# Softmax head steps: reciprocal of the row sums posted five half-steps later, the second projection copy recorded behind the exponentials, projection stores posted three half-steps sooner in the lead-in

## The chip, the cores and the metric

The kernel runs on one core of one Trainium2 chip. The metric is the device time of one execution in microseconds (us), the median of three runs. A profiled execution of the same program gives the span, the engines' busy times and every instruction's place; it is a fourth execution, with a time of its own. Engines are called as in the profile: PE (matmuls), PEld (its weight loads), DVE, ACT, POOL, and SP, which issues all the DMAs here.

## The reference

Four layers on x of 2048 x 640 in fp32, each added to its input: attention, Fourier mixing, attention, Fourier mixing.

```
def _A_ref(x, wqkv, wo):
    H = 32; Dh = D // H; W = 256
    qkv = (x @ wqkv).reshape(B, S, 3, H, Dh).transpose(2, 0, 3, 1, 4)
    ...
    scores = jnp.where(mask[None, None], scores, -1e9)   # 0 <= i - j < W
    p = _softmax(scores, axis=-1)
    o = jnp.einsum("bhqk,bhkd->bhqd", p, v)
    return o.transpose(0, 2, 1, 3).reshape(B, S, D) @ wo
def _B_ref(x, ...):   # Real(DFT_seq(DFT_hidden(x))) by four real matrices
    ...
x = x + _A_ref(_layernorm(x), A_wqkv, A_wo)
x = x + _B_ref(_layernorm(x), ...)
```

and the last two lines once more. The head width is 20, and a query sees the 256 keys up to its own.

## The kernel before

Every fp32 product is split into a high and a low part and made of three matmuls. The program is written out by hand: each engine executes its instructions in the order in which the Python code records them, and waits only where data or a buffer is not ready. All that the change touches lies in the attention layers, so it happens twice (about 126 to 620 us and 1240 to 1735 us of the profile).

**Head steps.** `heads` walks over 8 quads (four heads each) of 16 query blocks of 128 rows: 128 steps, with 10 steps of lead-in, numbered -10 to 128. A step has two half-steps, z = 0 and z = 1 (two heads each). Step t makes, for query block t + 10, the scores whose row maxima DVE takes (`s_head`, L548, and L553); for key block t, the transposed scores with the maximum folded in (`t_head`, L573), their exponentials on ACT (L582) and the window masks on POOL (L588, L592); and for block t - 1 the product with v (`pv`, L603). After every fourth block `finish` has the row sums of the exponentials gathered by a small DMA into `sm` (L623), DVE takes their reciprocal (L626), and a DMA stores it in `r_d` (L629), from where it is later read, broadcast, to scale the heads' outputs.

**Fill.** Between the heads' matmuls of z = 0 and z = 1 `fill` gives PE other work, taken in one sequence: first the q and k projections of the coming quads (`pieces`, L188 with 128x512 results), then 16 tiles of the output projection's first part (`partials`, L188 with 128x320 results, added up at L847), then 16 tiles of its second part (`late`, L170, added at L934 and L940). What the head steps have not done of it `after_heads` does afterwards, mixed with the first matmuls of the Fourier layer (`unit`, L1220). The second sequence can't begin before its first inputs are loaded and scaled: `prepare` asks at each step whether the reciprocals of quad 5, block 0 are stored (`others`, `self.stored`, set in `store`), and then loads, multiplies (L769) and splits (L163) them over the next 10 half-steps; until that is done (`made`, `early_o` in `more`), and once the projections are used up, a step has no fill at all.

**Copies.** A finished pair of projection results stands in PSUM banks 6 and 7 (`heavy`); `relieve` has ACT copy one to SBUF (L472, 128x512). One half-step later POOL makes the high part (L473), two half-steps later the low part (L474), and six half-steps later SP stores both in `qk_d` (L453). The destination `c` has three buffers, so a fourth cast waits until the first store has landed.

**Posting.** `post(d, fn)` puts an instruction off by d half-steps; `tick`, at the end of a half-step, records what has come due. So a delay is a place in the order, not a time.

Of the kernel before, what the change touches and what calls it, by code (L numbers as in the profile page):

```python
# [23 lines left out]
NQ = H // 4  # L24
# [37 lines left out]
class Net:  # L62
# [393 lines left out]
    def pieces(self, c, sbs, role):  # L456

        w = self.turn["w", c]
        sets, of = [], {}
        for sb in sbs:  # L460
            xt = self.xnt(sb)
            if sb % 2 == 0:
                sets.append(([], []))
            p = self.bank(role)
            of[id(p)] = p, sb, self.last_bank
            sets[-1][0].append(p)
            sets[-1][1].append([((w[:, 0, k, :], w[:, 1, k, :]), (xt[:, 0, k, :], xt[:, 1, k, :])) for k in range(KC)])

        def copied(p, sb):
            st = self.work.tile([P, 2, 512], F32R, name="c", tag="c", bufs=3)  # L470
            r = self.raw()[:, :512]
            self.nc.scalar.activation(r, p, AF.Copy)  # L472
            self.post(1, lambda: self.nc.gpsimd.tensor_copy(st[:, 0, :], r))  # L473
            self.post(2, lambda: self.nc.gpsimd.tensor_tensor(  # L474
                out=st[:, 1, :], in0=r, in1=st[:, 0, :].bitcast(F32), op=OP.subtract))
            self.post(6, lambda: self.store_qk(c, sb, st))
        for r in self.lockstep(sets):
            if isinstance(r, tuple):
                for p in r[1]:
                    p, sb, k = of[id(p)]  # L480
                    self.heavy.append((k, lambda p=p, sb=sb: copied(p, sb)))
                r = 0
            yield r
# [33 lines left out]
    def heads(self, xsrc, xdst, hook):  # L517
# [7 lines left out]
        def defer(d, fn):  # L525
            later.setdefault(now[0] + d, []).append(fn)
# [3 lines left out]
        def load_v(n):  # L530
            if n < 4 * NQ:
                nc.sync.dma_start(self.vq[n % 3][:, :384].rearrange("p (t c) -> p t c", c=96),
                                  self.vd[n // 4][:, n % 4 * 4:n % 4 * 4 + 4, :])
# [84 lines left out]
        def finish(quad, bk, ou):  # L618
            sm = pool.tile([P, 16], F32, name="sm", tag="sm")
            rc = pool.tile([P, 16], F32, name="rc", tag="rc")  # L620
            cols = slice(bk * 512, (bk + 1) * 512)
            at = (2, 7, 9) if quad < NQ - 1 else (1, 5, 6)
            self.post(at[0], lambda: nc.sync.dma_start(sm, ou[0:P:32, :]))  # L623
            self.post(at[0], lambda: nc.sync.dma_start(
                self.od[4 * quad:4 * quad + 4, :, cols].rearrange("h r s -> (h r) s"), ou))
            self.post(at[1], lambda: nc.vector.reciprocal(out=rc, in_=sm))  # L626

            def store():
                nc.sync.dma_start(  # L629
                    self.rd[bk, 4 * quad:4 * quad + 4, :].rearrange("h (a b) -> (h a) b", b=16), rc)  # L630
                self.stored.add((quad, bk))
            self.post(at[2], store)
# [15 lines left out]
        def relieve():  # L648
            while self.heavy:
                self.relieve()  # L650

        def more():

            r = next(self.proj, None)
            if r is not None:
                done[0] += r
                return r
            if not made[0] and self.early_o[0]["left"]:
                return None
            r = next(self.out, None)  # L660
            if r is not None:
                made[0] += r
                return r
            return next(self.rest, None) if self.left or self.ready_late() else None

        def fill(n):

            k, size = 0, 1
            while k < size:
                r = more()  # L670
                if r == 0 and k == 0:
                    continue
                if r != 1:
                    return
                k += 1
                if k == 1:
                    left = self.left + 1
                    size = -(-left // max(1, round(left / n)))
            if self.left == 0:
                more()  # L680
                relieve()

        load_v(0)
        load_v(1)
# [1 line left out]
        for step in range(-LEAD, steps + 1):  # L686
            now[0] = step
            self.wide, self.lead, self.tiled = step + LEAD > steps, step < -2, step < steps - 1
            for f in later.pop(step, []):
                f()  # L690
            s, t, v = step + LEAD, step, step - 1
            if due and s >= due[0][0]:
                while done[0] < due[0][1]:
                    fill(15)
                due.pop(0)
                q, j = (s + AHEAD) // 16, (s + AHEAD) % 16 // 4
                for i, f in enumerate(self.pack(q, j)):
                    defer(i // 3, f)
                for f in later.pop(step, []):
                    f()  # L700
            if v >= 0 and v % 4 == 3:
                load_v(v // 4 + 2)
            if done[0] < total:
                nf = max([FIRST if t < 0 else RATE]
                         + [(d - done[0]) / max(1, at - s) for at, d in due])
            elif made[0] < early:
                nf = LATE
            else:
                nf = LATE
            rows = ((s - 1) // 16, ((s - 1) % 16) // 4) if 4 <= s < steps + 4 and s % 4 == 0 else None  # L710
            for z in range(2):
                for e in range(2):
                    heads = [(t_head, t, e), (s_head, s, 1 - e)]
                    for head, n, i in heads[::-1] if e else heads:
                        if 0 <= n < steps:
                            head(n // 16, n % 16, z, i)
                if 0 <= t < steps:
                    for e in range(2):
                        t_exp(t // 16, t % 16, z, e, e + 1)
                    t_mask(t // 16, t % 16, z)  # L720
                if z:
                    if 0 <= v < steps:
                        pv(v // 16, v % 16)
                    if rows:
                        m_rows(*rows)
                if z == 0 and t >= 0 or t < -1 or t >= steps:
                    fill(nf)
                self.tick()
            if step >= steps:
                self.load_to(step - steps + 2)  # L730
            if step > 16 * (NQ - 1):
                self.poll_late(step - 16 * (NQ - 1))
# [794 lines left out]
```

## Time and profile before

| | us |
|---|---|
| median of 3 runs (lowest, highest) | 2259.83 (2257.31, 2260.46) |
| the profiled execution's own time | 2260.54 |
| its span, first to last instruction | 2258.8 |
| PE, DVE, ACT, POOL busy in the span | 2169.5, 1489.8, 1114.2, 1014.9 |
| mean granted TensorE clock | 0.987 |

The span is 1.7 us short of that execution's time. A row of the windows view is a stretch in us, its length, then for each engine its busy time with the count of instructions, then the granted TensorE clock as a part of full speed (PEclk), the DMA engines' busy share, and GB/s. A row of the timeline is start, length, engine, line, operation, names and count, and in brackets how long the engine was idle before it and what ended that. The ends of matmuls are modelled, so a busy PE need not be at its peak.

### The profile page before, as it was taken

The page shows a single profiled execution, that of the slowest core. Times are in us where ns is not written, and L with a number is a line of the kernel's source. Part 1 is how long each engine was busy: PE and PEld are TensorE (multiplying, and loading weights), DVE is VectorE, ACT ScalarE, POOL GpSimd, SP SyncE. Part 2 cuts the span into 40 slices and gives each one's busy share as a digit, 9 for nine tenths or more (in the row PEclk, how much of TensorE's full clock was granted, in tenths as well). Part 3 has the DMA queues.
Part 4 walks back from the last instruction along what each step waited for, and adds up shares of the span by engine and source line. Part 5 has one row for each costly group of instructions (what it writes and reads, how often), then busy time and mean ns, then how long its engine had stood idle before and what let it go on. Part 6 is the DMA issues. An engine that isn't in the chain of part 4 may idle for free. (4 is left out here: it accounts for less than half of the span.)

```text
span 2258.8 us, 49233 instructions
## 1 busy us (share of the span) xinstructions
PE 2169.5 (96%) x18064; PEld 1817.8 (80%) x18064; DVE 1489.8 (66%) x3705; ACT 1114.2 (49%) x2401; POOL 1014.9 (45%) x1540
## 2 busy tenths in 40 slices
PE   7999999998889999999999999999998899999999
PEld 7987777677768888889999777777776688888999
DVE  6347788674787868772461578876746968678522
ACT  2117777656454545541331277776655545446310
POOL 3037776767745223230130477678676433232200
PEclk9999999899999999999999999998999999999999
DMA  5545656775435353655446465668753354545553
GB/s 180 179 143 186 195 185 198 220 208 163 138 117 182 125 183 131 214 170 168 161 165 190 142 194 179 202 195 233 198 170 120 117 183 139 168 156 201 164 166 100
DMA packets 217297, 385.57 MB, mean 171 GB/s; under 512 B 38880, under 2 KB 85472, under 8 KB 217056
## 3 DMA queue, kind: packets, MB, share of 16 engines
q1 hardware_dynamic: 217056, 382.43, 53.2%
q8 instruction: 143, 2.34, 0.5%
q14 instruction: 98, 0.80, 0.1%
HBM read 267.39 MB, written 113.77 MB: 169 GB/s over the span
## 5 line engine op out<-in xcount | busy, mean ns | idle before, releaser
L553 DVE CUSTOM_DVE_ANT_0 banks<-banks,mask 128x384 f32<-128x384 f32 (+2 forms) x1024 | 526.7, 557 | 174.7 <-PE banks L548 125.7
L582 ACT ACTIVATE pt<-banks 128x384 f32<-128x384 f32 (+2 forms) x1024 | 430.8, 469 | 209.4 <-PE banks L548 115.0
L573 PE MATMUL banks<-qp,kp 61*128 61x384 f32 (+2 forms) x1024 | 320.0, 376 | 10.7 <-ACT pt L582 9.2
L588 POOL TENSOR_SCALAR_AFFINE_SELECT pt<-pt 128x256 f32<-128x256 f32 x512 | 208.1, 407 | 206.9 <-ACT pt L582 156.5
L548 PE MATMUL banks<-kp,qp 60*128 60x384 f32 (+2 forms) x1024 | 285.5, 367 | 11.4 <-DVE mc L553 10.7
L188 PE MATMUL banks<-big,wc 64*128 64x512 f32 x1920 | 266.9, 392 | 0.4 <-DVE pt L371 0.4
L573 PEld LDWEIGHTS banks<-qp,kp 61*128 61x128 f32 x1024 | 178.8, 187 | 78.6 <-ACT pt L582 43.9
L603 PE MATMUL banks<-pt,vq 128*32 128x128 f32 x5760 | 220.3, 281 | 8.8 <-POOL pt L588 8.8
L188 PEld LDWEIGHTS banks<-big,wc 64*128 64x128 f32 x1920 | 186.4, 186 | 20.1 <-DVE pt L371 0.5
L163 DVE TENSOR_TENSOR qp<-pt,qp 128x512 fp32r<-128x512 f32 (+1 forms) x209 | 167.7, 811 | 50.8 <-ACT qp L157 50.0
L603 PEld LDWEIGHTS banks<-pt,vq 128*32 128x32 f32 x5760 | 146.1, 111 | 67.1 <-issue 52.2
L548 PEld LDWEIGHTS banks<-kp,qp 60*128 60x128 f32 x1024 | 164.8, 188 | 32.9 <-DVE mc L553 23.6
L592 POOL TENSOR_SCALAR_AFFINE_SELECT pt<-pt 128x256 f32<-128x256 f32 x448 | 182.7, 408 | 0.0
L157 ACT ACTIVATE qp<-pt 128x512 fp32r<-128x512 f32 (+1 forms) x209 | 128.9, 624 | 104.6 <-DMA pt<-c 36.5
L1220 PE MATMUL banks<-qp,big 128*128 128x512 f32 x630 | 153.4, 394 | 6.1 <-POOL big L163 4.3
L1149 POOL TENSOR_TENSOR pt<-pt,pt 128x512 f32<-128x512 f32 x40 | 59.7, 1496 | 203.7 <-DMA pt<-c 134.8
L1408 DVE TENSOR_TENSOR x<-banks,x 128x320 f32<-128x320 f32 x64 | 29.8, 488 | 178.6 <-DMA x<-x_d 108.8
L553 DVE DVE_READ_ACCUMULATOR2_ANT mc<- 128x1 f32 x1024 | 144.9, 141 | 0.0
L1220 PEld LDWEIGHTS banks<-qp,big 128*128 128x128 f32 x630 | 118.2, 189 | 32.0 <-POOL big L163 5.8
L157 ACT ACTIVATE c<-pt 128x512 fp32r<-128x512 f32 x144 | 88.2, 624 | 74.9 <-DVE pt L1146 36.0
L163 DVE TENSOR_TENSOR c<-pt,c 128x512 fp32r<-128x512 f32 x140 | 112.3, 814 | 14.9 <-ACT c L157 12.6
L170 PE MATMUL banks<-big,pt 128*128 128x320 f32 x768 | 118.2, 309 | 0.9 <-DVE pt L1345 0.9
(201 smaller groups left out, 4430.5 us busy)
## 6 DMA issues: line engine op xcount, KB each, us to landing
pt<-c SPq DMA_DIRECT2D x188, 512.0 KB
qk_d<-c SPq DMA_DIRECT2D x80, 512.0 KB
kp<-qk_d SPq DMA_DIRECT2D x384, 80.0 KB
qp<-qk_d SPq DMA_DIRECT2D x384, 80.0 KB
kp<-u_d SPq DMA_DIRECT2D x32, 640.0 KB
o_d<-ou SPq DMA_DIRECT2D x64, 256.0 KB
x_d<-x SPq DMA_DIRECT2D x48, 320.0 KB
v_d<-pt SPq DMA_DIRECT2D x16, 768.0 KB
```

Of the source, the lines that this page charges most:

```text
L157: nc.scalar.activation(hi, src, AF.Copy, scale=-1.0 if neg else 1.0)
L163: (eng or nc.vector).tensor_tensor(out=lo, in0=src, in1=hi.bitcast(F32), op=OP.subtract)
L170: self.nc.tensor.matmul(p, x, y, start=n == 0, stop=n == last)
L188: self.nc.tensor.matmul(ps[a], x[r], y[r], start=half + i == 0, stop=half == 1 and i == n - 1, skip_group_check=True)
L548: nc.tensor.matmul(p, qp[quad % 2][b:b + 60, z, qb * P:(qb + 1) * P], kp[quad % 2][b:b + 60, z, k0 * P:(qb + 1) * P], start=True, stop=True)
L553: nc.vector.tensor_tensor_reduce(out=p, in0=p, in1=self.mask[:, 384 - n * P:], scale=1.0, scalar=NEG, op0=OP.add, op1=OP.max, accum_out=mc ...
L573: nc.tensor.matmul(self.banks[:, e, :n * P], kp[quad % 2][b:b + 61, z, kb * P:(kb + 1) * P], qp[quad % 2][b:b + 61, z, kb * P:(kb + n) * P ...
L582: nc.scalar.activation(pt[quad, kb][:, 2 * z + e0:2 * z + e1, :n * P], self.banks[:, e0:e1, :n * P], AF.Exp, scale=SCALE)
L588: nc.gpsimd.affine_select(out=t[:, :, 0:P], in_=t[:, :, 0:P], pattern=[[0, 2], [1, P]], compare_op=OP.is_ge, fill=0.0, base=0, channel_mul ...
L592: nc.gpsimd.affine_select(out=t[:, :, 256:384], in_=t[:, :, 256:384], pattern=[[0, 2], [-1, P]], compare_op=OP.is_gt, fill=0.0, base=0, ch ...
L603: nc.tensor.matmul(p[32 * h:32 * h + 32, :], vq[:, 96 * (kb % 4) + 21 * h:96 * (kb % 4) + 21 * h + 32], t[:, h, (qb - kb) * P:(qb - kb + 1 ...
L1220: nc.tensor.matmul(self.banks[:, bk, :], p, b[q], start=start and m == 0, stop=stop and last and m == 2, skip_group_check=True)
```

## The change

Four edits. In `finish`, for all quads but the last, the reciprocal is posted 12 half-steps after the block instead of 7, and its store (with the mark in `self.stored`) 14 instead of 9. At the end of `fill` one finished projection result is copied instead of all; the rest is copied in the next half-step z = 1, behind its exponentials and masks. In pieces that are begun in the lead-in, the store is posted 3 half-steps after the copy instead of 6.

```diff
--- before.py
+++ after.py
@@ -466,6 +466,8 @@
             sets[-1][0].append(p)
             sets[-1][1].append([((w[:, 0, k, :], w[:, 1, k, :]), (xt[:, 0, k, :], xt[:, 1, k, :])) for k in range(KC)])
 
+        lead = self.lead
+
         def copied(p, sb):
             st = self.work.tile([P, 2, 512], F32R, name="c", tag="c", bufs=3)
             r = self.raw()[:, :512]
@@ -473,7 +475,7 @@
             self.post(1, lambda: self.nc.gpsimd.tensor_copy(st[:, 0, :], r))
             self.post(2, lambda: self.nc.gpsimd.tensor_tensor(
                 out=st[:, 1, :], in0=r, in1=st[:, 0, :].bitcast(F32), op=OP.subtract))
-            self.post(6, lambda: self.store_qk(c, sb, st))
+            self.post(3 if lead else 6, lambda: self.store_qk(c, sb, st))
         for r in self.lockstep(sets):
             if isinstance(r, tuple):
                 for p in r[1]:
@@ -619,7 +621,7 @@
             sm = pool.tile([P, 16], F32, name="sm", tag="sm")
             rc = pool.tile([P, 16], F32, name="rc", tag="rc")
             cols = slice(bk * 512, (bk + 1) * 512)
-            at = (2, 7, 9) if quad < NQ - 1 else (1, 5, 6)
+            at = (2, 12, 14) if quad < NQ - 1 else (1, 5, 6)
             self.post(at[0], lambda: nc.sync.dma_start(sm, ou[0:P:32, :]))
             self.post(at[0], lambda: nc.sync.dma_start(
                 self.od[4 * quad:4 * quad + 4, :, cols].rearrange("h r s -> (h r) s"), ou))
@@ -678,7 +680,8 @@
                     size = -(-left // max(1, round(left / n)))
             if self.left == 0:
                 more()
-                relieve()
+                if self.heavy:
+                    self.relieve()
 
         load_v(0)
         load_v(1)
@@ -719,6 +722,7 @@
                         t_exp(t // 16, t % 16, z, e, e + 1)
                     t_mask(t // 16, t % 16, z)
                 if z:
+                    relieve()
                     if 0 <= v < steps:
                         pv(v // 16, v % 16)
                     if rows:
```

ACT, steps 3 and 4 (the first place after the lead-in with two copies): `x` is the copy's destination, `pt` the exponentials', `wc` a weight split. Before:

```order
L582 ACTIVATE pt_96<-banks 128x384 x2
L472 ACTIVATE x<-banks 128x512 x2
L582 ACTIVATE pt_96<-banks 128x384 x2
L582 ACTIVATE pt_93<-banks 128x384 x2
L157 ACTIVATE wc<-x 128x384
L582 ACTIVATE pt_93<-banks 128x384 x2
```

and with the change:

```order
L584 ACTIVATE pt_96<-banks 128x384 x2
L474 ACTIVATE x<-banks 128x512
L584 ACTIVATE pt_96<-banks 128x384 x2
L474 ACTIVATE x<-banks 128x512
L584 ACTIVATE pt_93<-banks 128x384 x2
L157 ACTIVATE wc<-x 128x384
L584 ACTIVATE pt_93<-banks 128x384 x2
```

The second copy now stands behind the two exponentials of z = 1 and ahead of those of the next step.

SP in the lead-in, from the load of the next weights: `qk_d<-c` are the projection stores, `qp<-mt` the row maxima, `kp<-qk_d` and `qp<-qk_d` the loads of the next quad. Before:

```order
L429 DMA x<-wqk 128x640
L564 DMA qp_104<-mt 2x4x128 x2
L453 DMA qk_d<-c 128x2x512 x4
L505 DMA kp_102<-qk_d 20x2x512 x3
L429 DMA x<-wqk 128x640
L564 DMA qp_104<-mt 2x4x128 x2
L505 DMA kp_102<-qk_d 20x2x512 x3
L453 DMA qk_d<-c 128x2x512 x2
L505 DMA qp_103<-qk_d 20x2x512 x3
L453 DMA qk_d<-c 128x2x512 x2
```

and with the change:

```order
L453 DMA qk_d<-c 128x2x512
L429 DMA x<-wqk 128x640
L453 DMA qk_d<-c 128x2x512 x2
L566 DMA qp_104<-mt 2x4x128 x2
L453 DMA qk_d<-c 128x2x512 x2
L507 DMA kp_102<-qk_d 20x2x512 x3
L429 DMA x<-wqk 128x640
L453 DMA qk_d<-c 128x2x512 x2
L566 DMA qp_104<-mt 2x4x128 x2
L507 DMA kp_102<-qk_d 20x2x512 x3
L453 DMA qk_d<-c 128x2x512
L507 DMA qp_103<-qk_d 20x2x512 x6
```

The first store now stands ahead of the weights' load, and seven of the eight ahead of the second `qp<-mt`; POOL's casts of the second results move half a step down in the same way.

PE at the end of the head steps, from step 127 on (`banks<-qp_104,kp_559` are late tiles of 12 matmuls each, `big,big` and `big` with 128x320 are partials, L1220 and L1224 the Fourier layer). Before:

```order
L170 MATMUL banks<-qp_104,kp_559 128x320 x12
L573 MATMUL banks<-qp_103,kp_102 128x128 x2
L603 MATMUL banks<-pt_93,vq_91 32x128 x4
L603 MATMUL banks<-pt_94,vq_91 32x128 x4
L603 MATMUL banks<-pt_95,vq_91 32x128 x4
L170 MATMUL banks<-qp_104,kp_559 128x320 x12
L603 MATMUL banks<-pt_94,vq_91 32x128 x4
L603 MATMUL banks<-pt_95,vq_91 32x128 x4
L603 MATMUL banks<-pt_93,vq_91 32x128 x4
L170 MATMUL banks<-qp_104,kp_559 128x320 x24
L1220 MATMUL banks<-qp_103,big_7889 128x512 x18
L170 MATMUL banks<-qp_104,kp_559 128x320 x12
```

and with the change:

```order
L605 MATMUL banks<-pt_93,vq_91 32x128 x4
L605 MATMUL banks<-pt_94,vq_91 32x128 x4
L605 MATMUL banks<-pt_95,vq_91 32x128 x4
L170 MATMUL banks<-big_5566,big_5569 128x320 x6
L170 MATMUL banks<-big_5566 128x320 x3
L605 MATMUL banks<-pt_94,vq_91 32x128 x4
L605 MATMUL banks<-pt_95,vq_91 32x128 x4
L605 MATMUL banks<-pt_93,vq_91 32x128 x4
L170 MATMUL banks<-big_5566,big_5569 128x320 x6
L170 MATMUL banks<-big_5566 128x320 x3
L170 MATMUL banks<-qp_104,kp_559 128x320 x60
L1224 MATMUL banks<-qp_103,big_7912 128x512 x18
```

Three late tiles have left the last two steps, and the last partial tile has come into them. It follows from the later mark in `self.stored`: counted over the steps, the first partial is recorded in step 98 instead of step 95, so that steps 92 to 97 have no fill where before steps 92 to 94 had none, and every partial stands three steps later.

## Prediction

> **What bounds the kernel now.** I read the page first, then windows over the attention's head steps, then the timeline where a window was slow.
>
> ```profile
> PE 2169.5 (96%) x18064; PEld 1817.8 (80%) x18064; DVE 1489.8 (66%) x3705; ACT 1114.2 (49%) x2401; POOL 1014.9 (45%) x1540
> core 0: us, PE busy (x) PEld busy (x) DVE busy (x) ACT busy (x) POOL busy (x), PEclk, DMA share, GB/s
> 300.00:400.00 100.00, 97.59 (x1367) 74.70 (x1363) 80.48 (x301) 75.53 (x188) 71.02 (x159) 1.00 0.61 191
> 400.00:500.00 100.00, 93.15 (x1290) 71.92 (x1291) 69.08 (x254) 61.95 (x152) 72.52 (x135) 0.91 0.75 212
> ```
>
> PE is the bound of the head steps, and the other engines gain or cost only where they make it stand still. Between 400 and 500 us it does so, and its granted clock falls to 0.91 on average. Three groups of the grouped lines name what the change aims at: DVE waits for the row sums in front of the reciprocal, POOL's cast for a projection store, PE's transposed scores for exponentials.
>
> ```profile
> L626 DVE RECIPROCAL rc<-sm 128x16 f32<-128x16 f32 x64 | 15.9, 248 | 10.8 <-DMA sm<-ou 10.7
> L473 POOL CAST c<-x 128x512 fp32r<-128x512 f32 x64 | 37.6, 612 | 51.1 <-ACT x L472 25.2 <-DMA qk_d<-c 18.5 <-ACT pt L582 7.0
> L573 PE MATMUL banks<-qp,kp 61*128 61x384 f32 (+2 forms) x1024 | 320.0, 376 | 10.7 <-ACT pt L582 9.2
> ```
>
> No instruction is added or removed but for the form of one partial tile in each attention; everything is order. I take the parts one by one, cutting windows at PE's first L573 of a step, so that a window is a step.
>
> **Stores sooner in the lead-in.** The timeline shows POOL's eighth cast waiting for the fifth result's store, POOL's masks behind it, and PE waiting for the masks; then steps 1 and 2 of the first attention, an undisturbed step (189.11), and step 1 of the second.
>
> ```profile
> 165.90 0.61 POOL L473 CAST c<-x 128x512 fp32r<-128x512 f32 x1 [7.10 <-DMA qk_d<-c]
> 168.95 0.42 POOL L588 TENSOR_SCALAR_AFFINE_SELECT pt<-pt 128x256 f32<-128x256 f32 x1
> 169.43 0.41 PE L603 MATMUL banks<-pt,vq 128*32 128x128 f32 x4 [1.64 <-POOL pt L588]
> 165.68:170.49 4.81, 2.87 (x26) 2.05 (x26) 2.80 (x12) 2.07 (x5) 4.59 (x8) 1.00 0.73 250
> 170.49:174.27 3.78, 3.78 (x37) 2.42 (x35) 2.28 (x8) 1.93 (x5) 2.77 (x8) 0.64 0.73 218
> 189.11:191.74 2.63, 2.63 (x45) 2.07 (x41) 2.04 (x8) 1.68 (x4) 1.53 (x4) 1.00 0.49 164
> 1286.98:1291.67 4.69, 2.87 (x26) 2.06 (x26) 2.80 (x12) 2.07 (x5) 4.59 (x8) 1.00 0.72 254
> ```
>
> With the store in front of the row maxima's DMAs on SP, it is issued as soon as POOL has made its low part, some 8 us before that cast. Behind it on SP stand the load of the next weights, which was issued long before it was used, and the row maxima of steps not yet begun; I cost both at nothing, covered by the 9 steps of lead-in, and if the cover failed it would be one such DMA late, once. The cast then goes through, POOL is free when the first exponentials come, and steps 1 and 2 take what the undisturbed step takes: (4.81 - 2.63) + (3.78 - 2.63) + (4.69 - 2.63) = 5.4 us gained. Bounds: nothing, if the cast stays late, to 5.4.
>
> **Reciprocals later.** Step 100 shows the wait: the gather is issued, lands 3.5 us later, DVE stands on the reciprocal, the score reductions queue behind it, and PE waits for their bank.
>
> ```profile
> 452.00 0.62 SPq L623 DMA_DIRECT2D sm<-ou  x1
> 455.50 0.25 DVE L626 RECIPROCAL rc<-sm 128x16 f32<-128x16 f32 x1 [3.58 <-DMA sm<-ou]
> 456.32 0.43 PE L548 MATMUL banks<-kp,qp 60*128 60x384 f32 x1 [2.70 <-DVE mc L553]
> 448.13:451.50 3.37, 3.29 (x50) 2.58 (x50) 2.33 (x9) 1.81 (x6) 3.37 (x6) 1.00 0.96 236
> 451.50:457.49 5.99, 3.29 (x56) 2.62 (x52) 2.41 (x10) 2.85 (x7) 5.57 (x9) 1.00 0.71 191
> 457.49:462.48 4.99, 4.80 (x54) 3.91 (x51) 3.09 (x12) 2.54 (x6) 2.74 (x6) 0.66 0.72 209
> 462.48:465.60 3.12, 3.12 (x56) 2.62 (x52) 1.98 (x11) 1.84 (x5) 1.55 (x5) 1.00 0.61 123
> 1569.25:1573.58 4.33, 3.29 (x56) 2.61 (x52) 2.41 (x10) 2.85 (x7) 4.33 (x6) 1.00 0.69 197
> 1573.58:1578.53 4.95, 4.77 (x55) 3.88 (x51) 3.11 (x12) 2.64 (x6) 3.99 (x9) 0.66 0.69 186
> 421.59:426.13 4.54, 3.32 (x34) 1.94 (x34) 2.32 (x9) 2.17 (x5) 4.54 (x8) 0.78 0.65 195
> 426.13:429.89 3.76, 3.44 (x38) 2.15 (x34) 2.28 (x8) 2.91 (x7) 3.76 (x7) 0.50 0.73 235
> ```
>
> The stall costs twice: in step 100, and in step 101, which runs at a clock of 0.66. Five half-steps are over 6 us at the shortest steps shown, more than the 3.58 that the longest wait lasted, so the wait goes. Step 100 becomes like step 99, step 101 like step 102: (5.99 - 3.37) + (4.99 - 3.12) in the first attention, (4.33 - 3.37) + (4.95 - 3.12) in the second. Step 92 of the first (4.54) has the same wait and becomes like step 93, 0.78. Together 8.1 us gained. The two buffers of `sm` and `rc` are enough, since the store is posted 14 half-steps after the block and a third block comes after 16. Bounds: 2.7 us, the one PE gap quoted, to 10.7 us of waits plus 3.7 us of slow clock.
>
> **What the later mark moves.** Quad 5's first reciprocals are marked 5 half-steps later, so the partials begin 3 steps later, and steps 95 to 97 lose their fill in both attentions. A step without fill is no shorter: 3.76 us, at a clock of 0.50, against 3.12 to 3.37 with fill. The step that opens the fill pays for the clock's return.
>
> ```profile
> 433.65:438.35 4.70, 4.70 (x53) 4.16 (x52) 2.07 (x7) 1.53 (x6) 0.98 (x3) 0.56 0.73 254
> 433.65:448.13 14.48, 14.37 (x179) 11.66 (x179) 10.26 (x36) 7.64 (x21) 5.11 (x14) 0.86 0.72 229
> 1552.69:1556.12 3.43, 3.43 (x52) 3.05 (x51) 1.83 (x7) 1.52 (x6) 1.64 (x5) 0.82 0.94 331
> 1552.69:1565.89 13.20, 13.12 (x180) 10.57 (x179) 10.21 (x36) 7.60 (x21) 5.85 (x16) 0.95 0.86 260
> 505.65:509.02 3.37, 3.29 (x51) 2.58 (x51) 2.33 (x9) 1.81 (x6) 3.37 (x6) 1.00 0.58 186
> 509.02:517.59 8.57, 7.04 (x104) 5.26 (x100) 7.00 (x22) 6.47 (x16) 8.57 (x13) 1.00 0.35 104
> ```
>
> Steps 95 to 98 now become three of 3.76 and one that opens: 3 x 3.76 + 4.70 - 14.48 = 1.5 us lost in the first attention, 3 x 3.76 + 3.43 - 13.20 = 1.5 in the second, 3.0 in all. Steps 116 and 117 (8.57, against twice 3.37) suffer because the last partials' splitting falls together with that of the late weights; three steps later it falls elsewhere. That could give back 1.8 us an attention; I take half, 1.8 in all, since the place where it falls is not seen.
>
> Behind PE's last L573 the order of before has 12 + 24 + 12 late matmuls up to the end of late tile 4, the changed one 9 + 9 of a partial and 60 late ones: 30 more in each attention. But there PE stood still anyway, waiting for POOL to split the next late inputs.
>
> ```profile
> 543.97 2.03 PE L170 MATMUL banks<-qp,kp 128*128 128x320 f32 x12
> 563.81 2.94 PE L170 MATMUL banks<-qp,kp 128*128 128x320 f32 x8 [1.09 <-POOL kp L163]
> 553.35:565.70 12.35, 8.13 (x27) 5.41 (x26) 5.70 (x13) 6.82 (x13) 12.12 (x11) 0.79 0.95 306
> ```
>
> At 2.03 / 12 = 0.17 us, 30 matmuls are 5.1 us; PE is idle 12.35 - 8.13 = 4.2 us in the window before that wait ends. With the late tiles recorded first, POOL's splitting of those inputs comes ahead of the work on normalized rows, so I take the idle time as filled: 0.9 us lost in each, 1.8 in all. Bounds: nothing, to 10.2 in all if PE's idle time stays, and 29 by the slow rival below.
>
> On the clock the row comes first: 0.50 in a step in which PE is busy 3.44 of 3.76 us. The Trainium skill, TensorE: Matmul & The Clock Gate, Part 1: The HAM clock gate, has the gate at half rate after an idle window of about 3.4 us and at full rate after a busy one. Read literally, a step with 0.3 us of idle time should run at full clock, like the 2.63 of the undisturbed step, and the six steps would give 6 x (3.76 - 2.63) = 6.8 us back, 2243; the row contradicts it, and I stay with 3.76.
>
> **The second copy behind the exponentials.** Rows of step 19: both copies, the exponentials behind them, PE's wait, the fill of step 20.
>
> ```profile
> 220.05 1.08 ACT L472 ACTIVATE x<-banks 128x512 f32<-128x512 f32 x2
> 221.02 0.88 ACT L582 ACTIVATE pt<-banks 128x384 f32<-128x384 f32 x2
> 221.57 0.44 PE L573 MATMUL banks<-qp,kp 61*128 61x384 f32 x1 [0.35 <-ACT pt L582]
> 222.04 0.65 PE L188 MATMUL banks<-big,wc 64*128 64x512 f32 x3
> ```
>
> Half a copy, 0.54, no longer delays the exponentials, so they end at about 221.4 and PE's 0.35 us of idle time goes. But the second copy then runs from 221.4 to 221.9, and it frees bank 7, which the next fill's second matmul writes. Without the wait that fill would begin 0.35 us before 222.04, about 221.7, and stand there until about 222. So PE's wait moves from the exponentials to the bank. POOL's work up to the masks of step 20 is the same sum in another order. I take nothing, between 9.2 us gained (all of L573's waits) and 24 x 0.35 = 8.4 lost, a bank wait at each of 24 groups on top of what is there.
>
> **The sum.** -5.4 - 8.1 + 3.0 - 1.8 + 1.8 + 0 = -10.5. The profiled execution took 2260.5, of which 1.7 lies around the span, and is 0.7 above the median; the sum gives **2250.0**.
>
> **Rivals.** (1) Slower: the three late tiles are paid at the pace of the chain behind them. In that stage two late tiles six apart end 29.6 us from each other, 4.9 each with its unit of Fourier matmuls.
>
> ```profile
> 581.40 0.88 DVE L940 TENSOR_TENSOR x<-banks,big 128x320 f32<-128x320 f32 x2
> 611.01 0.88 DVE L940 TENSOR_TENSOR x<-banks,big 128x320 f32<-128x320 f32 x2
> ```
>
> If each of the six tiles costs 4.9 instead of 0.3, that is 27.6 more: 2278. It decides from about 2.7 us a tile; against it stands that PE idles in the very place and that the first five tiles now run without units between them. Chance 0.12. (2) No change: those tiles cost PE's 5.1 us an attention without filling anything, nothing is gained at steps 116 and 117, and other stalls keep half the 8.1: 2250 + 8.4 + 1.8 + 4.0 = 2264, and 2258 with the first of these alone. For it: POOL is busy 12.12 of 12.35 there. Chance 0.16. (3) The copies give all 9.2: 2241. For it: ACT is less busy than PE; against it, the bank. Chance 0.12. (4) The clock as in the skill's section: by the rows above 6.8 less, 2243, chance 0.03. The forecast: 0.57.
>
> **The numbers.** About 0.2%, 4.5 us, is what a measurement of this kernel can tell from no change. Forecast, copies and clock are faster: 0.57 + 0.12 + 0.03 = 0.72; same 0.16, slower 0.12. The range reaches from the copies' case to the upper part of the second: 2241 to 2262.
>
> **What would show it.** Lead-in: the eighth cast without a DMA wait, steps 1 and 2 at 2.6. Reciprocals: no wait for `sm`, step 100 near 3.4, step 101 at full clock. Mark: six steps near 3.76 at clock 0.50 from step 92, first partial in step 98, late tile 4 of the first attention done within 3 us of before (565.7) after the other gains are taken off. Copies: L573's wait for ACT gone, a wait of L188 for ACT's copy in its place. The prediction is wrong if head steps with copies get shorter by more than 0.2, or if the stage after the heads grows by more than 3 us an attention.

## The result and the profile after

The changed kernel takes **2253.72 us** (median of nine executions, 2251.37 to 2256.64), the kernel before 2260.46 beside it; the ratio is 0.997 with a 95% interval of 0.9957 to 0.9984, so 3.6 to 9.7 us are gained (one disturbed execution of before is left out of it). 2250.0 had been forecast, 10.5 less. The profiled execution took 2251.37, with a span of 2249.6: it is the quickest of the nine, and its span is 9.2 us shorter than that of before, where the medians differ by 6.7. Of the 9.2, 1.1 lie ahead of the heads, in no row of the table below.

One profile is one execution. So the kernel before was profiled a second time (`r_before` below), and the table, summed from the steps' starts, has both. A step starts, here and in the prediction's windows, at its first score matmul (L548, L550 in the changed kernel); the prediction names L573 for it, which begins up to 0.45 us earlier. Each row is the sum of the two attentions.

| stage, us | forecast of its terms | before | before, second profile | after |
|---|---|---|---|---|
| steps 0 to 2 (stores) | -5.4 | 21.17 | 23.14 | 15.86 |
| steps 3 to 91 (copies) | 0 | 494.42 | 493.45 | 492.94 |
| steps 92 to 101 (reciprocals, lost fill) | -5.1 | 78.03 | 74.16 | 67.39 |
| steps 102 to 127 (collisions) | -1.8 | 167.46 | 168.18 | 172.25 |
| behind the heads, to the end of the layers | +1.8 | 1298.24 | 1303.18 | 1302.79 |

The stores and the copies came out as forecast. Steps 92 to 101 gave more than forecast, steps 102 to 127 took back what should have been a gain, and the stage behind the heads differs more between two profiles of one program (4.9 us) than the term that was to be seen in it.

Three groups of the grouped lines of the changed kernel, the same ones that the prediction shows of before (busy, mean ns of one, idle time in front of them and what ended it):

```profile
L628 DVE RECIPROCAL rc<-sm 128x16 f32<-128x16 f32 x64 | 15.5, 245 | 0.0
L475 POOL CAST c<-x 128x512 fp32r<-128x512 f32 x64 | 39.1, 612 | 33.9 <-ACT x L474 33.8
L575 PE MATMUL banks<-qp,kp 61*128 61x384 f32 (+2 forms) x1024 | 314.4, 374 | 21.0 <-ACT pt L584 14.5 <-DMA qp<-mt 5.1
```

The first two say that the change did what it was made for: no reciprocal waits for its sums any more (10.8 us before), no cast for a projection store (18.5). The third is the price: PE stands in front of its transposed scores for 21.0 us where it stood for 10.7, and 5.1 of it for a transfer that nothing waited for before.

Windows of the changed kernel: steps 1 and 2 of the first attention and step 1 of the second; steps 92, 95, 97 and 98; steps 100 and 101; steps 104 and 120.

```profile
164.61:167.34 2.73, 2.73 (x25) 2.13 (x26) 2.41 (x11) 2.07 (x5) 1.53 (x4) 1.00 0.82 295
167.34:169.93 2.59, 2.59 (x35) 2.02 (x34) 2.38 (x9) 1.93 (x5) 1.58 (x5) 1.00 0.58 162
1277.38:1280.09 2.71, 2.71 (x27) 2.14 (x27) 2.40 (x11) 2.07 (x5) 1.53 (x4) 1.00 0.79 265
416.35:418.98 2.63, 2.17 (x37) 1.45 (x33) 2.35 (x10) 2.28 (x6) 2.60 (x5) 1.00 0.48 145
424.41:426.72 2.31, 2.28 (x33) 1.33 (x33) 2.06 (x9) 1.52 (x6) 0.71 (x2) 1.00 0.91 337
429.34:435.14 5.80, 2.39 (x21) 1.23 (x18) 2.40 (x10) 3.16 (x7) 5.32 (x10) 0.71 0.75 269
435.14:439.66 4.52, 4.52 (x43) 3.95 (x44) 2.10 (x8) 1.84 (x5) 0.76 (x2) 0.62 0.60 179
442.85:446.12 3.27, 3.27 (x54) 2.57 (x51) 2.75 (x11) 1.70 (x5) 1.56 (x4) 1.00 0.96 275
446.12:449.14 3.02, 3.02 (x54) 2.56 (x51) 2.49 (x9) 2.14 (x6) 1.53 (x4) 1.00 0.65 189
456.00:460.44 4.44, 3.50 (x56) 2.76 (x52) 2.30 (x10) 2.26 (x5) 4.44 (x8) 1.00 0.66 185
509.85:515.64 5.79, 4.18 (x50) 2.94 (x46) 0.00 (x0) 2.37 (x5) 5.79 (x10) 0.83 0.78 243
```

Steps 1 and 2 take 2.6 to 2.7, as forecast, and steps 100 and 101 are at full clock. Steps 92 and 95 have no fill, and take 2.63 and 2.31 at a clock of 1.00, not 3.76 at 0.50. Then step 97 takes 5.80, and new long steps stand at 104 and 120 (112 and 119 are like them). The timeline shows what each waits for. First ACT and SP, then PE, at step 97:

```profile
424.61 0.25 ACT L564 ACTIVATE mt<-banks 16x128 fp32r<-16x128 f32 x1
431.57 1.31 SPq L566 DMA_DIRECT2D qp<-mt  x2
431.33 0.44 PE L575 MATMUL banks<-qp,kp 61*128 61x384 f32 x1 [1.37 <-ACT pt L584]
435.01 0.66 PE L575 MATMUL banks<-qp,kp 61*128 61x384 f32 x1 [2.04 <-DMA qp<-mt]
```

The negated row maxima `mt` are ready at 424.9, and their transfer is issued 6.7 us later, because SP's queue is that late. In step 104 and in step 120 it is another thing, seen in ACT's rows behind POOL's and in PE's:

```profile
456.50 1.30 POOL L773 TENSOR_TENSOR x<-x,rr 128x512 f32<-128x512 f32 x1
457.83 0.63 ACT L157 ACTIVATE big<-x 128x512 fp32r<-128x512 f32 x1 [2.00 <-POOL x L773]
458.89 0.44 PE L575 MATMUL banks<-qp,kp 61*128 61x384 f32 x1 [0.94 <-ACT pt L584]
510.86 1.28 POOL L773 TENSOR_TENSOR x<-x,rr 128x512 f32<-128x512 f32 x1
512.17 0.63 ACT L157 ACTIVATE big<-x 128x512 fp32r<-128x512 f32 x1 [2.50 <-POOL x L773]
513.23 1.05 PE L575 MATMUL banks<-qp,kp 61*128 61x384 f32 x2 [1.61 <-ACT pt L584]
```

ACT comes to the rounding of a normalized row (L157), which must wait for POOL's product (L773); the exponentials are behind it in ACT's order, and PE waits for those. So a chain of POOL, ACT and PE through an in-order queue has taken the place of the one through DVE.

### The profile page after: what moved, and what is told of

Same layout as the page of the kernel before. It is cut to its first block, busy times and chain, and to the rows that moved or that the text cites. A ratio compares the mean times of both kernels' runs of the same rounds, so it can differ in the third digit from the quotient of the medians.

```text
span 2249.6 us, 49097 instructions
## 1 busy us (share of the span) xinstructions
PE 2163.9 (96%) x18028; PEld 1807.9 (80%) x18028; DVE 1498.0 (67%) x3705; ACT 1112.7 (49%) x2401; POOL 1006.3 (45%) x1540
## 4 chain that ended last, share of the span: by engine, by line
PE 37%; POOL 5%; DVE 3%; ACT 2%; DMA 2%; issue 1%; SPq 0%; ACTq 0%; POOLq 0%; DVEq 0%
PE banks L1224 13%; PE banks L170 11%; PE banks L188 5%; PE banks L605 3%; PE banks L575 2%; PE banks L550 2%; POOL big L163 1%; POOL c L476 1%; ACT pt L584 0%; DMA qp<-qk_d 0%; POOL rs L952 0%; DMA rr<-r_d 0%; POOL kp L163 0%; DMA qk_d<-c 0%; ACT big L157 0%
## 5 line engine op out<-in xcount | busy, mean ns | idle before, releaser
L575 PE MATMUL banks<-qp,kp 61*128 61x384 f32 (+2 forms) x1024 | 314.4, 374 | 21.0 <-ACT pt L584 14.5
L550 PE MATMUL banks<-kp,qp 60*128 60x384 f32 (+2 forms) x1024 | 281.8, 361 | 1.3 <-DVE mc L555 1.1
L550 PEld LDWEIGHTS banks<-kp,qp 60*128 60x128 f32 x1024 | 161.4, 186 | 19.9 <-DVE mc L555 10.0
L157 ACT ACTIVATE c<-pt 128x512 fp32r<-128x512 f32 x150 | 93.3, 626 | 156.8 <-POOL pt L1142 52.1
L163 DVE TENSOR_TENSOR qp<-pt,qp 128x512 fp32r<-128x512 f32 (+1 forms) x191 | 156.0, 831 | 20.4 <-ACT qp L157 18.2
L157 ACT ACTIVATE qp<-pt 128x512 fp32r<-128x512 f32 (+1 forms) x195 | 120.2, 624 | 92.8 <-DVE pt L1154 35.7
L163 DVE TENSOR_TENSOR c<-pt,c 128x512 fp32r<-128x512 f32 x150 | 118.8, 802 | 65.5 <-ACT c L157 63.3
L1224 PE MATMUL banks<-qp,big 128*128 128x512 f32 x630 | 152.4, 394 | 7.3 <-ACT qp L157 3.4
L1224 PEld LDWEIGHTS banks<-qp,big 128*128 128x128 f32 x630 | 118.3, 190 | 33.5 <-ACT qp L157 4.2
L1224 PE MATMUL banks<-qp,xc 128*128 128x512 f32 x480 | 121.8, 400 | 7.9 <-DVE qp L163 6.7
```

Source lines behind the costliest of these rows:

```text
L157: nc.scalar.activation(hi, src, AF.Copy, scale=-1.0 if neg else 1.0)
L163: (eng or nc.vector).tensor_tensor(out=lo, in0=src, in1=hi.bitcast(F32), op=OP.subtract)
L550: nc.tensor.matmul(p, qp[quad % 2][b:b + 60, z, qb * P:(qb + 1) * P], kp[quad % 2][b:b + 60, z, k0 * P:(qb + 1) * P], start=True, stop=True)
L575: nc.tensor.matmul(self.banks[:, e, :n * P], kp[quad % 2][b:b + 61, z, kb * P:(kb + 1) * P], qp[quad % 2][b:b + 61, z, kb * P:(kb + n) * P ...
L1224: nc.tensor.matmul(self.banks[:, bk, :], p, b[q], start=start and m == 0, stop=stop and last and m == 2, skip_group_check=True)
```

## The experiments

Times are medians, ratios are against the kernel before in the same round of runs. Each kernel is the one named with the edit shown and nothing else; stages are from its profile.

**The stores alone** (before, with the sooner store):

```diff
+        lead = self.lead
...
-            self.post(6, lambda: self.store_qk(c, sb, st))
+            self.post(3 if lead else 6, lambda: self.store_qk(c, sb, st))
```

> The kernel before with the earlier store in the lead-in alone. Theory of the forecast: steps 1 and 2 of the heads fall to about 2.6 in both attentions and nothing else moves, 5.4 us less in all (3.3 in the first attention, 2.0 in the second). Rival: the gain is eaten up before step 12 by a later wait in the same queue, and the time stays within 1.5 us of before.

2253.90 us, ratio 0.9967 (0.9955 to 0.998): 4.5 to 10.2 us gained. Steps 0 to 2 take 7.78 and 7.83, as in the changed kernel. The forecast's term is right, and this edit alone is worth about as much as the whole change.

**The reciprocals alone** (before, with the later reciprocal):

```diff
-            at = (2, 7, 9) if quad < NQ - 1 else (1, 5, 6)
+            at = (2, 12, 14) if quad < NQ - 1 else (1, 5, 6)
```

> The kernel before with the reciprocal and its store five half-steps later, alone. Theory of the forecast: 8.1 gained by the waits, 3.0 lost by the later mark, 1.8 gained at steps 116 and 117, 1.8 lost behind the heads, 5.1 us less in all. Rival, read from the trace after the whole change: the wait of step 97 for the row of negated maxima, the waits at steps 104, 112 and 119 to 120 and the longer stage behind the heads give nearly all of it back, and only about 1.4 us are left. Both expect steps 92 to 96 at full clock if it was the wait of step 92 that halved it.

2257.52 us, ratio 0.999 (0.9979 to 1.0001). Between the two, and not told from nothing by its interval, which ends at 4.7 us gained: the forecast's 5.1 for this part lies outside it. Its profile has the pattern of the changed kernel step for step: steps 92 to 96 at 2.3 to 2.6, step 97 at 6.29 and 6.76, waits in steps 104, 112, 119 and 120.

**The copies alone** (before, with the second copy in z = 1):

```diff
-                relieve()
+                if self.heavy:
+                    self.relieve()
...
                 if z:
+                    relieve()
```

> The kernel before with the second projection copy behind the exponentials, alone (both halves of that edit). Theory of the forecast: nothing, within 1 us; PE's wait moves from the exponentials to the bank that the copy frees. Rival: the copies are worth 3 us or more, and the changed kernel's total hides it because another edit loses more than its share.

2258.84 us, ratio 0.999 (0.9979 to 1.0001): at most 4.7 us. Where the copies stand, in steps 3 to 91, the profile shows little: they take 492.9 us in both attentions, 1.5 and 0.5 less than in the two profiles of before. But steps 0 to 2 take 19.0 where before has 21.2 and 23.1: POOL's cast waits 5.0 us for the projection store in the first lead-in and not 7.1. So alone the edit gains 2 us or more there, which the forecast had not seen. In the changed kernel nothing of that is left, since the sooner store takes the wait away (15.9 for steps 0 to 2, and 15.6 with the stores alone). How the wait moved in the other steps shows in three of them with two copies, first of before, with its fill of step 20, then of the changed kernel, whose fills of steps 20 and 21 stand below.

```profile
218.53:227.79 9.26, 8.57 (x121) 6.43 (x120) 7.24 (x27) 7.77 (x20) 8.40 (x16) 1.00 0.51 152
222.04 1.30 PE L188 MATMUL banks<-big,wc 64*128 64x512 f32 x8
```

```profile
214.06:223.38 9.32, 8.73 (x119) 6.27 (x119) 7.14 (x26) 7.66 (x20) 8.39 (x16) 1.00 0.62 198
```

```profile
217.15 1.54 PE L188 MATMUL banks<-big,wc 64*128 64x512 f32 x8
220.22 1.09 PE L188 MATMUL banks<-big,wc 64*128 64x512 f32 x8
```

Step 19 loses its wait of 0.35, and the fill of step 20 takes 1.54 where it took 1.30 before (the next fill, of eight matmuls too, takes 1.09): its second matmul begins when the copy has freed the bank. Three steps together are 9.26 before and 9.32 after.

**The partials sooner** (the changed kernel, quad 5's first block alone at the old delays):

```diff
             at = (2, 12, 14) if quad < NQ - 1 else (1, 5, 6)
+            if (quad, bk) == (5, 0):
+                at = (2, 7, 9)
```

> The changed kernel, with the first block of quad 5 alone kept at the early reciprocal (7 half-steps) and early store (9), so that the partials may begin in step 95 as before while all waits for the reciprocals stay away. If the lost fill and the later start of the partials are what the change gives back, the wait of step 97 and those of steps 104, 112, 119 and 120 go or shrink, the stage behind the heads is as long as before, and the time is 3 to 9 us below the changed kernel's. Rival: the waits only move to other steps, since the same work of POOL and ACT meets the exponentials in another step, and the time is within 2 us of the changed kernel's.

2254.64 us, ratio 0.9972 (0.9961 to 0.9983): the rival. The waits of steps 97, 104, 112, 119 and 120 are gone, and others stand in their place. The first of them in step 94, ACT's rounding and then PE:

```profile
423.74 0.63 ACT L157 ACTIVATE big<-x 128x512 fp32r<-128x512 f32 x1 [1.38 <-POOL x L775]
424.96 0.63 ACT L157 ACTIVATE big<-x 128x512 fp32r<-128x512 f32 x1 [0.59 <-POOL x L775]
425.92 0.58 PE L575 MATMUL banks<-qp,kp 61*128 61x256 f32 x1 [2.85 <-ACT pt L584]
```

So where the partials begin decides in which steps POOL's products collide with the exponentials, and in this pair of kernels not how much it costs.

**The rounding later** (the changed kernel, 11 or 12 half-steps after the load in place of 10; POOL's low part is recorded with the rounding and moves with it; 12 is shown):

```diff
-        eng, at = (nc.vector, (6, 8)) if self.after else (nc.gpsimd, (8, 10))
+        eng, at = (nc.vector, (6, 8)) if self.after else (nc.gpsimd, (8, 12))
```

> The changed kernel, with the rounding and splitting of normalized rows posted 11 in place of 10 half-steps after the load, so that ACT comes to the rounding half a step later and has less to wait for POOL's product. Theory, ACT stands in front of the exponentials waiting for POOL: the waits at steps 104, 112, 119 and 120 (0.94, 0.80, 0.43 and 1.61 us) shrink by half or more, 2 to 4 us an attention, 4 to 8 us below the changed kernel. Rival, POOL's own work sets the pace: the waits only move to other steps, within 2 us of the changed kernel.

> The same with 12 in place of 10 half-steps. Theory: the waits at steps 104, 112, 119 and 120 and ACT's part of the wait in step 97 (1.4 us) go, about 5 us an attention with the slow clock behind the longest, 7 to 10 us below the changed kernel in all. Rival: POOL sets the pace and the waits move, within 2 us; or the inputs of the next partials are now late for PE, and the time is above the changed kernel's.

With 11: 2241.38 us, ratio 0.9922 (0.9906 to 0.9938), 12.3 less than the changed kernel, and 10.8 by the ratios, since the two ran in different rounds. With 12: **2238.97 us, 0.9911** (0.9894 to 0.9929), 14.7 less, 13.3 by the ratios. The theory holds, and more than its upper end (8 and 10) is gained both times. Steps 117 to 127 of the changed kernel and of the one with 12, then two of ACT's roundings in step 105 of the latter, without a wait:

```profile
500.00:535.33 35.33, 33.23 (x495) 26.97 (x495) 9.61 (x28) 23.20 (x58) 28.16 (x51) 0.95 0.48 150
```

```profile
498.29:530.07 31.78, 31.75 (x486) 26.06 (x486) 10.66 (x29) 22.98 (x58) 28.11 (x51) 1.00 0.51 155
```

```profile
458.68 1.14 ACT L157 ACTIVATE big<-x 128x512 fp32r<-128x512 f32 x2
```

POOL has the same work in both (28.1 us) and PE stands still for 2.1 us in the one and 0.03 in the other. ACT's part of the wait in step 97 is gone too; the transfer's part has grown:

```profile
435.44 0.65 PE L575 MATMUL banks<-qp,kp 61*128 61x384 f32 x1 [3.98 <-DMA qp<-mt]
```

**The row of maxima on another queue** (the changed kernel, the two transfers that step 97 waits for):

```diff
+                eng = nc.scalar if (quad, u) == (6, 1) else nc.sync
-                self.post(1, lambda z=z: nc.sync.dma_start(
+                self.post(1, lambda z=z, eng=eng: eng.dma_start(
```

> The changed kernel, with the two transfers of the row of negated maxima that step 97 waits for (quad 6, second half) issued on ACT's queue in place of SP's, where they stand behind the loads of the partials. Theory, SP's queue is late there: the waits of 2.0 us in the first and 3.0 us in the second attention go, steps 92 to 98 get 2 to 3 us shorter in each, and the time is about 5 us below the changed kernel's. Rival, the stretch ends with POOL's and ACT's work on the new partials, whatever PE waits for first: another wait takes the place of this one, and steps 92 to 98 get less than 1 us shorter.

2260.29 us, ratio 1.0002 (0.9992 to 1.0012): the rival, and worse than it. Steps 92 to 98 take 27.18 and 26.22 where the changed kernel takes 23.31 and 25.05. Rows of ACT and PE:

```profile
425.69 1.67 ACTq L567 DMA_DIRECT2D qp<-mt  x2
427.79 0.47 PE L576 MATMUL banks<-qp,kp 61*128 61x128 f32 x1 [1.87 <-ACT pt L585]
```

Issuing the two takes ACT 1.67 us in front of the exponentials, PE waits 1.87 for those, and step 96 behind it takes 3.76, at a clock of 0.50. The Trainium skill, DMA: Bandwidth & Descriptors, Issuing engines are not separate DMA queues, says that transfers issued from different engines run on the same DMA engines and that another issuer saves only the time to issue. In this trace that time was not saved but moved to ACT, the 1.67 us; on which DMA engines the two transfers ran, no row here shows.

**The same program twice.**

> The kernel before once more, unchanged, for a second profile: how far the same program differs between two profiled executions, stage by stage. Theory: steps 92 to 101 differ by 1 to 3 us and the stage behind the heads by up to 3 us, since transfers set both; all other stages agree within 0.3 us. Rival: every stage agrees within 0.5 us, and the 1.3 and 3.2 us by which the stage behind the heads is longer in the changed kernel are the change's.

2259.77 us, ratio 1.0005 (0.9993 to 1.0018). Steps 92 to 98 differ by 2.3 and 1.0 us between the two profiles, the stage behind the heads by 2.7 and 2.3, steps 0 to 2 by 0.5 and 1.5 and the start ahead of the heads by 1.1, which the theory had not said. So the 1.3 and 3.2 us of that stage are not shown to be the change's. Steps 92 to 94 of this second profile of before (first attention):

```profile
420.25:422.87 2.62, 2.36 (x32) 1.55 (x32) 2.15 (x9) 2.08 (x5) 2.62 (x5) 1.00 0.53 162
422.87:425.49 2.62, 2.16 (x36) 1.37 (x32) 2.21 (x10) 2.13 (x5) 2.62 (x6) 1.00 0.82 236
425.49:431.34 5.85, 3.09 (x37) 1.94 (x33) 2.39 (x10) 2.74 (x7) 5.85 (x8) 0.80 0.87 275
```

Here the wait of step 92 happened to be 0.26 us, and the steps without fill take 2.62 at full clock, with step 94 paying for it. Steps 92 and 93 of the kernels with the stores and with the copies alone, which have the same work there, take 2.6 to 3.0 in both attentions. The 3.76 of the first profile was no property of such a step.

**Rounding later and the partials sooner** (both edits above):

> The changed kernel with the rounding 12 half-steps after the load, and the first block of quad 5 alone at the early reciprocal and store, so that the partials may begin 3 steps sooner. If the steps without fill cost time of their own (3.0 us by the forecast), it is 3 us or more below the kernel with the later rounding alone (2239). Rival: the stretch from step 92 to 98 ends with its transfers, and the late tiles behind the heads have idle time to stand in, so that the place of the fill is indifferent: within 2 us of 2239.

2248.14 us, ratio 0.9938 (0.9925 to 0.995): neither. It is some 6 us above the later rounding alone by their ratios. Steps 92 to 98 are 2.2 us longer in its profile, the stage behind the heads 6.4, of which 4.9 are seen between profiles of one program. So the later start shows no cost of its own in the total; why the sooner start costs more stays open.

**The residual rows later** (the changed kernel with the rounding at 12, and the first four loads of 320 KB two, then five steps later):

```diff
-            self.load_y(range(AHEAD_X))
+            self.defer(2, lambda: self.load_y(range(AHEAD_X)))
```

> The changed kernel with the rounding 12 half-steps after the load, and the first four loads of the residual rows two steps later, behind the row of negated maxima in SP's queue. Theory, SP's queue stands for these loads and the row comes late: the wait of step 97 (3.98 and 2.95 us with the later rounding alone) falls below 1 us in both attentions, and the time is 4 to 6 us below 2239. Rival: the other transfers are as late, another wait takes its place (as where the row went to ACT's queue), within 2 us of 2239 or above.

Two steps later: 2242.86 us, ratio 0.9918 (0.9904 to 0.9931), no better than 0.9911, and the waits are longer. Rows of SP and PE:

```profile
426.88 2.61 SPq L827 DMA_DIRECT2D big<-x  x4
432.22 1.29 SPq L566 DMA_DIRECT2D qp<-mt  x2
437.64 0.66 PE L575 MATMUL banks<-qp,kp 61*128 61x384 f32 x1 [4.25 <-DMA qp<-mt]
```

The loads had come to stand right ahead of the row, and it was in flight for more than 5 us. With five steps they stand behind it:

> The changed kernel with the rounding 12 half-steps after the load, and the first four loads of the residual rows five steps later, so that in SP's queue they stand behind the row of negated maxima that step 97 waits for, and not just ahead of it, as they did two steps later (waits of 4.25 and 5.75 us). Theory, these loads are what delays the row: the wait of step 97 falls below 1 us in both attentions, and the time is 3 to 6 us below 2239. Rival: the loads only meet the next transfers that PE needs, another wait of the same size takes its place by step 102, within 2 us of 2239.

**2234.62 us, ratio 0.9889** (0.9869 to 0.9909), the best of all: 1.1% below before. The row is issued at 427.5 and the loads at 432.6, no wait for it is left, and steps 92 to 98 take 19.28 us (first attention; 22.86 with the later rounding alone, 23.31 in the changed kernel):

```profile
427.52 1.52 SPq L566 DMA_DIRECT2D qp<-mt  x2
432.62 2.31 SPq L827 DMA_DIRECT2D big<-x  x4
```

```profile
416.40:435.68 19.28, 16.14 (x208) 9.90 (x204) 15.98 (x60) 14.06 (x37) 16.79 (x32) 0.94 0.76 234
```

So it was these loads that made the row late. By the ratios 5.0 us are gained on the later rounding alone, though the two intervals overlap; step 99 behind the stretch takes 5.00 in place of 3.54.

**The later rounding without the change** (before, with 12 half-steps):

> The kernel before with the later rounding (12 half-steps) alone. If the waits at steps 100, 101, 108, 116 and 117 of before were ACT's wait for POOL and not the reciprocals, they go without the change: 8 to 10 us below before in all, and with the change's stores (5.4) that makes up the whole distance to 2239, about 2246. If DVE's wait for the sums of the block is a cause of its own, step 100 keeps a wait of 1 to 2.7 us in each attention, and it stays above 2250.

2253.47 us, ratio 0.996 (0.9946 to 0.9974). Both theories hold in part: the waits at steps 108, 116 and 117 go (steps 117 to 127 of the first attention take 31.55 in place of 32.81), step 100 of the first attention takes 3.27 with the reciprocals where they were, and a wait for the sums remains in step 100 of the second attention, in DVE's row and PE's:

```profile
1567.57 0.25 DVE L626 RECIPROCAL rc<-sm 128x16 f32<-128x16 f32 x1 [3.68 <-DMA sm<-ou]
1568.39 0.52 PE L548 MATMUL banks<-kp,qp 60*128 60x384 f32 x1 [3.02 <-DVE mc L553]
```

The rounding gains 8.2 us without the change and some 13 with it by the ratios. That would mean that each is worth more with the other, but the intervals overlap (5.9 to 12.2 us without the change), so that is not shown.

## Why the prediction was right, and where it was wrong

- **Stores**: right in mechanism and size. -5.4 forecast, -5.3 and -7.3 against the two profiles of before, and 4.5 to 10.2 alone.
- **Reciprocals**: right for the waits themselves. No reciprocal waits, and steps 100 and 101 take 3.27 and 3.02 at full clock. But the wait in step 100 is not the reciprocal's alone: with the later rounding in before, it is gone from the first attention of that profile, and 3.02 us long in the second. And what the later reciprocals bring in all, with everything that hangs on them, was forecast at -5.1 and measures -4.7 to +0.2 by themselves.
- **"A step without fill is no shorter: 3.76 us, at a clock of 0.50"**: wrong, and the first step that failed. The row was that of a step behind a wait: steps 92 and 93 in the second profile of before, with 0.26 us of wait in step 92, run at 1.00 in 2.62, and steps 92 to 96 of the changed kernel at 1.00 in 2.3 to 2.9. The clock rival was right as far as these steps go, against the row I held up to it. What the quicker steps win is largely paid back in step 97, where SP's queue is late (5.80 and 6.78); the two together are 10.6 us less than the first profile of before in steps 92 to 101 and 6.8 less than the second, where 5.1 was forecast. The kernel with the partials sooner has the fill back and is 0.9 us from the changed one, with other waits in the place of step 97's: the lost fill shows no cost of its own in the total.
- **"Three steps later it falls elsewhere. That could give back 1.8"**: wrong in sign, and the term that made the total too good. Steps 116 and 117 are indeed undisturbed, 1.15 and 0.99 shorter, but steps 104, 112, 119 and 120 wait instead, and steps 102 to 127 are 4.8 and 4.1 us longer than in the two profiles of before. The cause is shown by the later rounding: not the late weights, as I had put it, but ACT waiting for POOL's product in front of the exponentials.
- **Late tiles behind the heads**: no sign of the slow rival in the place it was to be seen. DVE adds up late tile 4 of the first attention from 549.92 on, 14.6 us behind PE's last matmul of the heads (535.33), without a wait; before it was 19.5 behind (565.72, heads to 546.25), after one of 4.32. The stage as a whole is 0.4 us shorter than in the second profile of before and 4.6 longer than in the first, so a term of 1.8 can't be seen in it. The mark that I set, 3 us an attention, was passed in the second (3.2), and an unchanged program comes to 2.3 there.

```profile
549.92 0.97 DVE L944 TENSOR_TENSOR x<-banks,big 128x320 f32<-128x320 f32 x2
```

```profile
565.72 0.49 DVE L940 TENSOR_TENSOR x<-banks,big 128x320 f32<-128x320 f32 x1 [4.32 <-PE banks L170]
```

- **Copies**: right for the change as a whole, and for the reason given: PE's waits for the exponentials go (2.6 us in steps 9 to 89 of the first attention before, none after), the wait goes to the bank, and POOL's masks take the rest (3.6 us of PE's waits in five of these steps, 2.3 before). The whole fill of step 20 grew from 1.30 to 1.54. What the edit gives alone in steps 0 to 2 was not foreseen.

The total, 2250.0 against 2253.72, is 3.7 us off, and lies within the range. It is near for the stores, which by themselves give as much as the whole, and by luck for the rest: against the two profiles of before, 1.7 to 5.5 us more are gained than forecast in steps 92 to 101, and 5.9 to 6.6 are missing in steps 102 to 127.

## What to carry to other kernels

A wait that is taken out of an in-order queue uncovers the next one in another queue, so ask for each engine what it would stand at if it came there earlier: here ACT at a rounding whose input POOL had not made, and SP behind loads that nobody needed yet. A delay in half-steps is tuned for the collisions that it was made among; move one, and the others of the same chain (here 10 to 12 for the rounding) are worth trying again. And a slow step behind a stall says nothing about its kind until a second execution without the stall has been seen.

## What the runs showed of the hardware

The granted clock goes by windows of 3.41 us, and not by the idle share of a step. In before, its second profile and the changed kernel every change of the granted clock stands on a grid of 3.41 us, and the low stretches of the head steps are one to four such windows long (3.41, 6.83, 10.24 or 13.65 us). In before, the window from 420.69 to 424.10, with PE busy for 1.95 us, is followed by 13.65 us at half clock. The rows show a stretch close to it and the first 10 us behind it:

```profile
420.60:424.00 3.40, 2.01 (x30) 1.14 (x27) 1.69 (x8) 2.67 (x7) 3.40 (x7) 1.00 0.85 242
424.00:434.00 10.00, 9.46 (x94) 5.93 (x95) 6.04 (x23) 5.68 (x14) 9.81 (x15) 0.51 0.72 220
```

The windows of steps 92 to 96 in the changed kernel, with PE busy for 2.93 to 3.05 of 3.41 us, stay at 1.00, as do those with the waits of 0.94 and 0.80 us in steps 104 and 112 (busy for 72% and 76%). The window with step 120's wait of 1.61 us, busy for 53%, is followed by one at half clock, and so is that with step 97's first wait (60%). There is no single limit in these profiles: in the head steps the clock fell behind windows with 19% to 73% of PE busy, and stayed full behind others with 54% and 65% to 73%.

The Trainium skill, TensorE: Matmul & The Clock Gate, Part 1: The HAM clock gate, has a half rate after an idle window of about 3.4 us and the full one after a busy window of that length. The grid agrees with that length. The fall agrees if a window at 57% counts as idle; the return in before does not come after the first three windows of these head steps, in which PE shows as busy for 3.09, 3.27 and 3.40 of 3.41 us, but after the fourth, which the dense fill of step 95 takes up from 434.25 on.

That SP stands for loads is the program's doing as far as the trace shows. Its DMAs tell of their landing by eight semaphores used in turn, and an issue waits until the transfer eight issues ahead of it, with the same semaphore, has landed. In before, SP stood 2.9 us ahead of a store of outputs, until one of the residual loads had landed, the one eight issues ahead. Rows of SP:

```profile
430.90 0.62 SPq L623 DMA_DIRECT2D sm<-ou  x1
434.41 0.34 SPq L624 DMA_DIRECT2D o_d<-ou  x1
```
